# Attention and expert layer: the planner learns that engines share a PSUM bank one at a time

## The chip, the cores and the metric

The kernel runs on one core of a Trainium2 chip. The metric is the time of one execution on the device in microseconds (us). Three runs of the kernel before took 918.87, 920.80 and 922.08 us, a median of 920.8 us.

The names of the engines in profiles: PE is TensorE's matmul, PEld its weight load, DVE is VectorE, ACT is ScalarE, POOL is GpSimd and SP is SyncE, which here issues the DMAs.

## The reference

An attention over 8 batches, 8 heads, 576 positions and 64 channels is followed by a two-layer network on 4608 tokens of 512 channels (hidden width 2048). Half of the heads see the last 32 positions, the other half every 32nd.

```python
scores = scale * np.matmul(q, k.transpose(0, 1, 3, 2))
mask_local = (rel >= 0) & (rel < stride)
mask_strided = (rel >= 0) & (pos[None, :] % stride == pos[:, None] % stride)
scores = np.where(masks[None, :, :, :], scores, -1000000000.0)
attn = np.exp(scores - np.max(scores, axis=-1, keepdims=True))
attn = attn / (np.sum(attn, axis=-1, keepdims=True) + 1e-09)
x = np.matmul(attn, v)               # then (B * S, H * D)
h = x @ w_in
sp = np.maximum(h, 0.0) + np.log1p(np.exp(-np.abs(h)))
g = h * erf(sp)
return (g @ w_out).astype(np.float32)
```

## The kernel before

Every value of the network is split into a high part, which TensorE multiplies at full rate, and a low part for the rest; a product of two such values is three matmuls (high by high, high by low, low by high).

The work has four stretches. In the head (up to about 46 us) the attention of the first two batches is computed (`head`), while the weights arrive by DMA and are split. In the second stretch (to about 267 us) three chunks of 384 tokens go through the network tile by tile (`ftile`): mm1 fills a bank `h`, VectorE and ScalarE make the gate from it in some nine alternating steps (n1 to split_lo), and mm2 multiplies the result with `w_out`. Then come six phases of 512 tokens (`phase`), each of eight pair groups (`pair_group`), 48 in all, to about 834 us; the attention of the later batches runs between them (`quad`, `attend`, `products`). A last chunk of 384 tokens ends the kernel (`tail`).

A pair group computes two tiles of the hidden layer with seven products in place of eight, by a scheme of Strassen's kind. It uses two PSUM banks, g[0] and g[1], each with a left and a right half of 256 columns:

- mmA (TensorE) writes both halves of g[0], mmB both halves of g[1]; each is 12 matmuls of 256 columns.
- save1 (ScalarE) copies g[0] left into `tmp`. mix1 (VectorE) adds g[0] right and writes `tmp` (called `spare` in the profile).
- mix3 (VectorE) writes g[0] right from g[1] right. mix2 writes g[1] left, save2 (ScalarE) copies it, mix4 writes g[1] right.
- mmC (6 matmuls) adds to g[0] left; it needs save1 and mmB. mmD (6) adds to g[0] right; it needs mix3. mmE (6) adds to g[1] left; it needs save2 and mix4.

After that both banks are gated like the tiles of a chunk, with 512 columns, and mm2 takes the first 384 tokens of each (three blocks of three matmuls a tile), while the last 128 are put aside for mmL. In the profile mmA to mmE are L1229, mix1 to mix4 L1238, save1 and save2 L1244, mm2 is L1397 (in chunks L961), mmL L1272, mm1 L894; the gating steps on VectorE are L1347, L1358 and L1368 (in chunks L905, L929 and L935).

All operations are first recorded in a plan, with an engine, a duration that the author gave, the operations they come after and the buffers they use. Five PSUM banks are shared by all tiles of the tags in `SHARED` (`ps`, `s`, `t`, `h`, `g`, `d`). `ORDER`, a table of 4669 numbers, gives each engine a queue of its operations. `Plan.order` then lets the planned time run: at each step it asks `_ready` when the first operation of each queue could begin, starts the one that can begin earliest, and returns all operations by their planned start. In that order they are written into the program, with `keep_in_program_order`, and there the layer below puts in the semaphores: an instruction waits for those written before it with which it shares a buffer. While the planned TensorE has nothing to do before the first mm1, `order` fills in a warm matmul (L1525).

Of the kernel before, what the change touches and what calls it, by code (L numbers as in the profile page):

```python
# [65 lines left out]
class Buf:  # L66


    def __init__(self, tag, make):
        self.tag, self.make, self.users = tag, make, []  # L70
        self.tile = self.bank = None
# [29 lines left out]
SHARED, NBANK = {"ps", "s", "t", "h", "g", "d"}, 5  # L101


class Op:
    def __init__(self, eng, dur, emit, after, new, use, earliest):
        self.eng, self.dur, self.emit, self.earliest = eng, dur, emit, earliest
        self.after, self.new = list(after), list(new)
        self.start = self.end = None
        self.behind, self.slack = [], 0.0
        self.locks = eng == "pool" or eng == "dve" and emit.__name__ in TWO  # L110
        for b in self.new + list(use):
            b.users.append(self)

    def pools(self):
        return {p for b in self.new for p in ((b.tag, "bank") if b.tag in SHARED else (b.tag,))}


class Plan:

    ENGINES = ("pe", "act", "dve", "pool", "sp")
    SAME = {"pe": 0.0, "act": 0.14, "dve": 0.13, "pool": 0.1, "sp": 0.0}
    LATENCY = {"pe": 0.25, "act": 0.2, "dve": 0.15, "pool": 0.6, "sp": 0.1}
# [14 lines left out]
    def _ready(self, op, live, last):  # L140
        t = max([op.earliest, *(last[p] for p in op.pools())])
        if any(p.end is None for p in op.behind):
            return None
        for p in op.after:
            if p.end is None:
                return None
            t = max(t, p.end + (self.SAME if p.eng == op.eng else self.LATENCY)[op.eng])
        for i, b in enumerate(op.new):
            order = live.setdefault(b.tag, [])
            n = len(order) - self.bufs[b.tag] + sum(x.tag == b.tag for x in op.new[:i])  # L150
            if n >= 0:
                for u in order[n].users:
                    if u.end is None:
                        return None
                    t = max(t, u.end + (self.SAME if u.eng == op.eng else self.LATENCY)[op.eng])
        need = sum(b.tag in SHARED for b in op.new)
        if need:
            free = sorted(self._vacant(op.eng))
            if len(free) < need:
                return None  # L160
            t = max(t, free[need - 1][0])
        return t + op.slack
# [85 lines left out]
def attention_moe(  # L248
# [1286 lines left out]
    held, sync = None, mybir.DependencyInfo(mybir.DependencyClass.Sync, mybir.DependencyReason.DATA)  # L1535
    for op in plan.order(ORDER):
        for x in op.new:
# [142 lines left out]
```

## Time and profile before

| what | before |
|---|---|
| median of three runs | 920.8 us |
| profiled execution | 919.72 us |
| its span, from the first to the last instruction | 917.9 us |
| TensorE busy | 896.8 us, 98% |
| VectorE busy | 763.6 us, 83% |
| ScalarE busy | 637.5 us, 69% |
| granted TensorE clock, mean | 1.000 |
| chain that ended last | PE 72%, DVE 19%, ACT 6% |

The busy time of TensorE is a sum of pipelined matmuls with modelled ends; a matmul of 512 columns shows some 0.39 us, while the next one starts after 0.23 us. A stall therefore shows less in the busy share than in the distance between starts and in the idle time of the weight loads (PEld), which run ahead of the matmuls. A row such as `[0.27 <-DVE spare L1238]` says that the engine stood idle for 0.27 us before this instruction, and which instruction ended that.

### The profile page before, as it was taken

The numbers are of one execution on the slowest core, as the hardware profiler recorded it, in microseconds if no ns is written. First come the engines' busy times: TensorE is split into PE (matmuls) and PEld (weight loads), VectorE is DVE, ScalarE is ACT, GpSimd is POOL, SyncE is SP. The second block draws the span as 40 slices with busy tenths as digits, with TensorE's granted clock in tenths as the row PEclk, the third lists the DMA queues.
The fourth block names the chain that finished last, engine by engine and source line by source line (L and its number), as shares of the span: only waits on it lengthen the run. The fifth ranks groups of instructions, "written<-read, shape, count | busy, mean of one in ns | idle before, by whom it ended". The sixth has DMA issues, their size and how long they took to land.

```text
span 917.9 us, 20199 instructions
## 1 busy us (share of the span) xinstructions
PE 896.8 (98%) x7530; PEld 780.2 (85%) x7530; DVE 763.6 (83%) x1669; ACT 637.5 (69%) x1484; POOL 348.1 (38%) x208
## 2 busy tenths in 40 slices
PE   9999999999989999999999999999999999999998
PEld 7889999888878887888788888888888888888997
DVE  6899989998998888889988889888988986774453
ACT  4877777676766776686667776876677677775554
POOL 4631363156663435464354446524356131000000
PEclk9999999999999999999999999999999999999999
DMA  9987746536748654585646764856577646553531
GB/s 359 363 312 203 228 148 209 157 95 190 219 166 270 216 182 174 204 265 185 219 171 226 239 199 120 300 164 217 161 234 240 196 152 192 188 184 115 173 114 46
DMA packets 90721, 183.51 MB, mean 200 GB/s; under 512 B 8704, under 2 KB 37888, under 8 KB 90624
## 3 DMA queue, kind: packets, MB, share of 16 engines
q1 hardware_dynamic: 90480, 182.12, 61.0%
q8 instruction: 59, 0.97, 0.4%
q14 instruction: 38, 0.31, 0.1%
q10 hardware_dynamic: 144, 0.11, 0.0%
HBM read 151.53 MB, written 30.67 MB: 198 GB/s over the span
## 4 chain that ended last, share of the span: by engine, by line
PE 72%; DVE 19%; ACT 6%; issue 2%; DMA 1%; DVEq 0%; ACTq 0%
PE ps L1229 20%; PE eo L1397 14%; PE ps L894 12%; PE o L961 12%; PE ps L1272 5%; DVE ps L1238 2%; PE warm L1525 2%; DVE glo_t L1368 2%; ACT ga L1353 1%; DVE ps L774 1%; DVE ga L1347 1%; PE ps L618 1%; DVE ps L1358 1%; ACT spare L1353 1%; DVE spare L1347 1%
## 5 line engine op out<-in xcount | busy, mean ns | idle before, releaser
L1397 PE MATMUL eo<-pair,ghi_t 128*128 128x512 f32 x576 | 181.8, 397 | 0.0
L1229 PE MATMUL ps<-T,st 128*128 128x256 f32 x1152 | 160.4, 285 | 3.8 <-DVE ps L1238 3.2
L1229 PEld LDWEIGHTS ps<-T,st 128*128 128x128 f32 x1152 | 149.0, 191 | 12.6 <-DVE ps L1238 6.6
L1229 PE MATMUL ps<-B,st 128*128 128x256 f32 x864 | 130.3, 289 | 8.1 <-DVE ps L1238 2.5
L1229 PEld LDWEIGHTS ps<-B,st 128*128 128x128 f32 x864 | 115.0, 190 | 26.8 <-DVE ps L1238 9.6
L961 PE MATMUL o<-pair,ghi 128*128 128x512 f32 x384 | 121.0, 396 | 0.0
L659 POOL PARTITION_ALL_REDUCE su_True<-sm_True x36 | 90.4, 2533 | 64.0 <-ACT sm_True L653 20.1
L908 ACT ACTIVATE ga<-ga 128x384 f32<-128x384 f32 x192 | 98.4, 523 | 23.0 <-DVE ga L905 21.4
L1397 PE MATMUL eo<-pair,glo_t 128*128 128x512 f32 x288 | 112.3, 390 | 0.0
L1397 PEld LDWEIGHTS eo<-pair,ghi_t 128*128 128x128 f32 x576 | 99.3, 189 | 14.0
L1353 ACT ACTIVATE ga<-ga 128x512 f32<-128x512 f32 x144 | 91.1, 633 | 15.3 <-DVE ga L1347 13.2
L1353 ACT ACTIVATE spare<-spare 128x512 f32<-128x512 f32 x144 | 91.1, 633 | 9.9 <-DVE spare L1347 8.3
L659 POOL PARTITION_ALL_REDUCE su_False<-sm_False x36 | 90.5, 2560 | 19.2 <-ACT sm_False L653 7.9
L639 POOL PARTITION_ALL_REDUCE mx_False<-sm_False x36 | 51.2, 1452 | 117.4 <-DVE sm_False L633 108.2
L639 POOL PARTITION_ALL_REDUCE mx_True<-sm_True x36 | 51.5, 1443 | 111.0 <-DVE sm_True L633 47.2
L1238 DVE TENSOR_TENSOR ps<-ps,spare 128x256 f32<-128x256 f32 x144 | 61.6, 429 | 35.8 <-PE ps L1229 29.2
L905 DVE SCALAR_TENSOR_TENSOR ga<-ga,ps 128x384 f32<-128x384 f32 x128 | 69.4, 547 | 23.7 <-ACT ga L908 22.4
L961 PEld LDWEIGHTS o<-pair,ghi 128*128 128x128 f32 x384 | 70.1, 188 | 12.4 <-ACT ghi L932 0.5
L961 PE MATMUL o<-pair,glo 128*128 128x512 f32 x192 | 75.9, 395 | 1.1 <-DVE glo L935 1.1
L894 PE MATMUL ps<-xhi,pair 128*128 128x384 f32 x384 | 75.5, 338 | 1.2 <-DVE sm_False L633 1.1
L1347 DVE SCALAR_TENSOR_TENSOR ga<-ga,ps 128x512 f32<-128x512 f32 x96 | 65.1, 678 | 10.1 <-ACT ga L1353 9.9
L1244 ACT COPY spare<-ps 128x256 f32<-128x256 f32 x96 | 35.7, 372 | 54.3 <-DVE ps L1238 48.8
(128 smaller groups left out, 1751.4 us busy)
## 6 DMA issues: line engine op xcount, KB each, us to landing
st<-ws SPq DMA_DIRECT2D x152, 512.0 KB, 4.7
st<-ws SPq DMA_DIRECT2D x64, 256.0 KB, 4.2
words<-w_out SPq DMA_DIRECT2D x16, 512.0 KB, 6.8
words<-w_in SPq DMA_DIRECT2D x16, 512.0 KB, 7.1
ws<-pair SPq DMA_DIRECT2D x64, 128.0 KB, 3.7
qk_True<-qk_loc SPq DMA_DIRECT2D x18, 416.0 KB, 5.1
out<-eob SPq DMA_DIRECT2D x24, 256.0 KB, 4.1
qk_False<-qk_str SPq DMA_DIRECT2D x12, 472.0 KB, 5.5
```

Source lines behind the costliest of these rows:

```text
L639: yield nc.gpsimd.partition_all_reduce(mx[k][:, :cols], sm[k][:, :cols], P, ReduceOp.max)
L659: yield nc.gpsimd.partition_all_reduce(su[k][:, :cols], sm[k][:, :cols], P, ReduceOp.add)
L894: yield nc.tensor.matmul(ph[:, :CH], weights(s, cc, w, fs), x[cc // 2][:, cc % 2, :], start=(i == 0), stop=(i == len(terms) - 1))
L905: yield nc.vector.scalar_tensor_tensor(out=out, in0=in0, scalar=scalar, in1=in1, op0=op0, op1=op1)
L908: yield nc.scalar.activation(dst, src, func, bias=bias[i], scale=scale)
L961: yield nc.tensor.matmul(po[:, half], g[:, ts], wout[f][:, w, half], start=(f == fs0 and i == 0), stop=(f == fs1 and i == 2 and half.stop ...
L1229: yield nc.tensor.matmul(slot(m, i), st[q][:, b, k, w], blk[x][:, y, k], start=first and t == k == 0, stop=True, skip_group_check=True,)
L1238: yield nc.vector.tensor_tensor(out=out(), in0=slot(*psum), in1=tmp[:, part], op=op)
L1272: yield nc.tensor.matmul(dps[0][:, :], x, wout[f][:, w, :], start=f == 0 and i == 0, stop=f == NFC - 1 and i == 2,)
L1347: yield nc.vector.scalar_tensor_tensor(out=a.tile, in0=a.tile, scalar=scalar, in1=ph[:, :TT], op0=ALU.mult, op1=ALU.add)
L1353: yield nc.scalar.activation(a.tile, ph[:, :TT] if i == 0 else a.tile, AF.Tanh, bias=bias[i], scale=scale)
L1397: yield nc.tensor.matmul(po.tile, x[:, ts], wout[f][:, w], start=f == 0 and i == 0, stop=f == NFC - 1 and i == 2)
```

## The change

`_ready` gets a rule: an operation that uses a shared bank may not be planned to start before the operations of other engines that were already started on that tile have ended, whichever part of the bank they touch. Before, only the operations named in `after`, and the handing over of a bank to a new tile, were planned for. The program's semaphores keep such pairs apart in the order they are written, before as now. With the new rule another `ORDER` was sought, a permutation of the same 4669 numbers; 273 places hold the same number as before.

```diff
-ORDER = (5, 229, 4667, 4, 4668, 131, 249, 230, 9, 21, 250, 231,
...
+ORDER = (1, 5, 229, 4, 39, 4667, 230, 4668, 249, 131, 210, 6,
...
@@ -110,6 +110,7 @@
         self.locks = eng == "pool" or eng == "dve" and emit.__name__ in TWO
         for b in self.new + list(use):
             b.users.append(self)
+        self.banks = [b for b in use if b.tag in SHARED]
...
@@ -153,6 +154,10 @@
                     if u.end is None:
                         return None
                     t = max(t, u.end + (self.SAME if u.eng == op.eng else self.LATENCY)[op.eng])
+        for b in op.banks:
+            for u in b.users:
+                if u.end is not None and u.eng != op.eng:
+                    t = max(t, u.end + self.LATENCY[op.eng])
         need = sum(b.tag in SHARED for b in op.new)
         if need:
             free = sorted(self._vacant(op.eng))
```

All lines behind it have numbers that are 5 higher in the new kernel (L1229 is L1234, L1238 is L1243, L1397 is L1402).

The order of TensorE, in the last pair group of the first phase. `st0` to `st2` hold the group's weights: st0 is mmA (its second half is the first row here), st1 mmB, st2 with B21 mmC and with B22 mmD; the rows that write `eo` are mm2, three matmuls to a block. Before:

```order
L1229 MATMUL ps3_98<-T2_0_3532,st0_0_7_4442 128x256 x6
L1397 MATMUL eo0_0_3852<-pair26_1973,ghi_t0_10_4488 128x512 x2
L1397 MATMUL eo0_0_3852<-pair26_1973,glo_t0_10_4501 128x512
L1229 MATMUL ps0_95<-T3_0_3601,st1_0_7_4470 128x256 x6
L1229 MATMUL ps0_95<-T1_0_3434,st1_0_7_4470 128x256 x6
L1229 MATMUL ps3_98<-B21_0_3556,st2_0_7_4499 128x256 x6
L1229 MATMUL ps3_98<-B22_0_3647,st2_0_7_4499 128x256 x6
L1397 MATMUL eo2_0_3863<-pair26_1973,ghi_t0_10_4488 128x512 x2
L1397 MATMUL eo2_0_3863<-pair26_1973,glo_t0_10_4501 128x512
```

Now:

```order
L1234 MATMUL ps3_98<-T2_0_3543,st0_0_7_4448 128x256 x6
L1234 MATMUL ps2_97<-T3_0_3644,st1_0_7_4460 128x256 x6
L1234 MATMUL ps2_97<-T1_0_3471,st1_0_7_4460 128x256 x6
L1402 MATMUL eo1_0_3897<-pair26_1984,ghi_t0_10_4486 128x512 x2
L1402 MATMUL eo1_0_3897<-pair26_1984,glo_t0_10_4499 128x512
L1402 MATMUL eo0_0_3855<-pair26_1984,ghi_t0_10_4486 128x512 x2
L1402 MATMUL eo0_0_3855<-pair26_1984,glo_t0_10_4499 128x512
L1234 MATMUL ps3_98<-B21_0_3565,st2_0_7_4496 128x256 x6
L1234 MATMUL ps3_98<-B22_0_3557,st2_0_7_4496 128x256 x6
L1402 MATMUL eo2_0_3838<-pair26_1984,ghi_t0_10_4486 128x512 x2
L1402 MATMUL eo2_0_3838<-pair26_1984,glo_t0_10_4499 128x512
```

One block of mm2 stood between mmA and mmB and none between mmB and mmC; now none stands before mmB and two stand behind it. mmC and mmD follow each other as before, and behind them come mm2 and mmE.

The order of VectorE in the same group. The row that writes `spare` from `ps3` is mix1; those of the same line behind it are mix3, mix2 and mix4; L1347 and L1358 (now L1352 and L1363) are gating steps of other tiles. Before:

```order
L1358 TENSOR_TENSOR ps2_97<-ga_93,ps2_97 128x512
L1238 TENSOR_TENSOR spare_3651<-ps3_98,spare_3651 128x256
L1238 TENSOR_TENSOR ps3_98<-ps0_95,spare_3651 128x256
L1238 TENSOR_TENSOR ps0_95<-ps0_95,spare_3651 128x256
L1171 TENSOR_TENSOR B11_1_4567<-x01_3116,B11_1_4567 128x512
L1358 TENSOR_TENSOR ps1_96<-spare_3651,ps1_96 128x512
L1238 TENSOR_TENSOR ps0_95<-ps0_95,spare_3651 128x256
```

Now:

```order
L1243 TENSOR_TENSOR spare_3642<-ps3_98,spare_3642 128x256
L1352 SCALAR_TENSOR_TENSOR spare_3642<-spare_3642,ps4_99 128x512
L1243 TENSOR_TENSOR ps3_98<-ps2_97,spare_3642 128x256
L1243 TENSOR_TENSOR ps2_97<-ps2_97,spare_3642 128x256
L674 STREAM_TRANSPOSE tt_3_True_1_4567<-su0_3_True_1_4453 128x384
L1363 TENSOR_TENSOR ps1_96<-ga_93,ps1_96 128x512
L651 TENSOR_TENSOR sm0_3_True_2_4359<-sm0_3_True_2_4359,mx0_3_True_2_4517 128x384
L678 TENSOR_SCALAR r_3_True_1_4585<-tt_3_True_1_4567 128x12
L682 RECIPROCAL r_3_True_1_4585<-r_3_True_1_4585 128x12
L1243 TENSOR_TENSOR ps2_97<-ps2_97,spare_3642 128x256
```

mix1, mix3 and mix2 stand in the same sequence; a gating step now comes between mix1 and mix3, and four more rows between mix2 and mix4. What a row of one engine doesn't show is how it stands to the other engine's: in the program before, mix3 of this group is written behind mmC, now ahead of it. So it is in 35 of the 48 groups before and in 15 now; mmC follows directly on mmB in 30 groups before and in 13 now.

The number of warm matmuls before the first mm1 is 122 before and 115 now. No other instruction of TensorE, VectorE or ScalarE is added or taken away.

## Rows read from the trace of the kernel before

**Rows 1.** The page, part 1: engine, busy us (share of the span), instructions.
```profile
PE 896.8 (98%) x7530; PEld 780.2 (85%) x7530; DVE 763.6 (83%) x1669; ACT 637.5 (69%) x1484; POOL 348.1 (38%) x208
```

**Rows 2.** Waits of TensorE's weight loads, whole span: us in total, times, longest.
```profile
PEld ps L1229 <- DVE ps L1238: 16.2, 40, 1.5
...
PEld ps L1229 <- DVE spare L1238: 6.0, 14, 0.9
...
PEld ps L1229 <- issue: 3.0, 8, 0.9
```

**Rows 3.** Timeline, TensorE, one pair group: start, us, what [idle before <-releaser].
```profile
341.79 0.88 PE L1229 MATMUL ps<-B,st 128*128 128x256 f32 x6
342.50 0.88 PE L1229 MATMUL ps<-T,st 128*128 128x256 f32 x6
...
343.92 1.59 PE L1229 MATMUL ps<-T,st 128*128 128x256 f32 x12
345.77 0.97 PE L1229 MATMUL ps<-B,st 128*128 128x256 f32 x6 [0.27 <-DVE spare L1238]
347.27 0.98 PE L1229 MATMUL ps<-B,st 128*128 128x256 f32 x6 [0.53 <-DVE ps L1238]
```

**Rows 4.** Timeline, VectorE, the same stretch.
```profile
345.30 0.42 DVE L1238 TENSOR_TENSOR spare<-ps,spare 128x256 f32<-128x256 f32 x1
346.79 0.90 DVE L1238 TENSOR_TENSOR ps<-ps,spare 128x256 f32<-128x256 f32 x2 [1.07 <-PE ps L1229]
```

**Rows 5.** Timeline, weight loads, the same stretch.
```profile
345.77 0.77 PEld L1229 LDWEIGHTS ps<-B,st 128*128 128x128 f32 x6 [0.47 <-DVE spare L1238]
347.27 0.78 PEld L1229 LDWEIGHTS ps<-B,st 128*128 128x128 f32 x6 [0.73 <-DVE ps L1238]
```

**Rows 6.** Timeline, TensorE, another pair group.
```profile
598.35 0.63 PE L1397 MATMUL eo<-pair,ghi_t 128*128 128x512 f32 x2
...
599.05 0.62 PE L1397 MATMUL eo<-pair,ghi_t 128*128 128x512 f32 x2
...
599.74 1.59 PE L1229 MATMUL ps<-B,st 128*128 128x256 f32 x12
```

**Rows 7.** Timeline, VectorE, the same stretch.
```profile
598.15 0.39 DVE L1238 TENSOR_TENSOR spare<-ps,spare 128x256 f32<-128x256 f32 x1
598.64 0.90 DVE L1238 TENSOR_TENSOR ps<-ps,spare 128x256 f32<-128x256 f32 x2
```

**Rows 8.** Line L1238 by itself: count, ns min/median/max, first and last start.
```profile
L1238 DVE TENSOR_TENSOR ps<-ps,spare x144: 401/432/433, 278.2 to 834.3; 128x256 f32<-128x256 f32 x144
```

**Rows 9.** Timeline, ScalarE, the stretch of rows 3.
```profile
347.72 0.37 ACT L1244 COPY spare<-ps 128x256 f32<-128x256 f32 x1 [0.56 <-DVE ps L1238]
```

**Rows 10.** Timeline, all engines, 436 to 439 us.
```profile
436.24 2.78 POOL L659 PARTITION_ALL_REDUCE su_False<-sm_False  x1 [0.16 <-DVE tt_False L669]
...
436.57 1.58 DVE L673 TENSOR_SCALAR r_False<-tt_False 128x9 f32<-128x9 f32 x1
...
438.78 0.38 PE L1229 MATMUL ps<-T,st 128*128 128x256 f32 x1 [1.31 <-DVE ps L1238]
```

**Rows 11.** Timeline, TensorE, where the pair groups begin.
```profile
273.99 0.68 PE L618 MATMUL ps<-qk_False 64*64 64x54 f32 x30 [2.33 <-DVE glo L935]
...
275.90 1.70 PE L1229 MATMUL ps<-T,st 128*128 128x256 f32 x12 [0.34 <-DVE sm_False L633]
```

**Rows 12.** Chain that ended last, up to 47 us: shares, then start, us, what.
```profile
by line: PE warm L1525 34.7%; PE ps L488 17.0%; PE av L500 16.7%; PE ps L391 9.5%; PE ps L471 7.3%; PE ps L535 4.6%; PE ps L500 2.9%; DVE sm L415 2.5%; PE ps L376 1.0%; DVE xn L526 0.7%; issue 0.4%; DVE cap L1528 0.4%; DVE r L515 0.4%; DVE 
...
41.24 2.29 PE warm L1525 x21
```

**Rows 13.** Stretches: us, busy (x) of each engine, clock, DMA share, GB/s.
```profile
0.00:46.00 46.00, 44.94 (x519) 35.55 (x520) 35.18 (x86) 30.89 (x92) 24.00 (x19) 1.00 0.96 360
...
267.00:834.00 567.00, 552.72 (x4982) 478.66 (x4982) 482.18 (x1062) 398.88 (x923) 225.94 (x115) 1.00 0.63 203
```

**Rows 14.** Waits of VectorE, whole span: us in total, times, longest.
```profile
DVE ps L1238 <- PE ps L1229: 29.2, 36, 5.4
```

2 lines of the change are left out of this document (1 added, 1 removed).

## The prediction

> **What bounds the kernel now.** I read the page's busy times first, then who the matmul engine waits for, then two stretches of the timeline, and last the order of the instructions. TensorE is busy for 98% of the span, every other engine for less [rows 1], so time can be won only where TensorE does not start its next matmul in time. Its matmuls are pipelined and their ends are modelled, so I take the idle time of the weight loads: a load that has to wait delays its matmul by nearly as much. The summary of these waits names one line above all: the matmuls of L1229 (the pair groups, mmA to mmE) wait 16.2 us in 40 places for a VectorE step of L1238 that writes `ps` (mix2 to mix4) and 6.0 us in 14 places for the one that writes `spare` (mix1); 3.0 us in 8 places end by nothing that the profile names [rows 2]. These 25 us are the stock from which this change can draw.
>
> The group at 341.8 us shows what the waits are [rows 3, 4]. mmB starts at 343.92 with 12 matmuls; at the 0.72 us for six that the rows of mmA show (341.79 to 342.50), mmC could start at 345.35. It starts at 345.77: mix1 ends at 345.72 (345.30 + 0.42). mmC reads and writes only the left half of bank g[0], and mix1 reads its right half; the two share nothing but the bank, and still the matmul is held until the VectorE step is over. Then mix3 (first of the two at 346.79) begins only when mmC's last matmul has ended (345.77 + 0.97 = 346.74); again they share only the bank. mmD truly needs mix3 and starts at 347.27, 0.78 us after mmC could have let it in. So 1.2 us are lost, and the two loads show idle times of 0.47 and 0.73 us [rows 5], the same sum. The holds are in the program, in the order in which it was written out; the planner of before did not know them.
>
> The group at 594.1 us shows the other way [rows 6, 7]: after mmB two blocks of mm2 follow (598.35 and 599.05, 0.69 us each), mix1 and then mix3 (in the pair at 598.64, over at 599.54) run beside them, and mmC and mmD follow at 599.74 as one row of 12 matmuls without a gap.
>
> **The change part by part.** No instruction of the real work is added or removed; the rule gives the planner the holds that the chip already carries out, and the numbers of ORDER give another order. So the sum is made from the places that moved.
>
> 1. *mix3 ahead of mmC.* Matching the rows of the order with the trace, before has mix3 behind mmC in 35 of the 48 groups and before it in 13; the change has it behind in 15 and before it in 33. Directly after mmB, with no other block, mmC stands in 30 groups before and in 13 now. The pieces of the order in the section on the change show it: two blocks of mm2 went from both sides of the group to between mmB and mmC. Of the load waits, the 35 groups carry the 14 for mix1 (6.0 us), 26 of the 40 for `ps` (9.6 us, all before mmD; the second of rows 5 is one) and 1.4 us of smaller ones: 17.0 us, 0.49 us a group. The 13 groups carry 3.5 us, 2.2 of it among the 8 without a name: 0.27 us a group. Twenty groups change sides: 20 x 0.22 = 4.3 us less. Bounds: nothing, if the wait only moves on to mmE; 17 us, if all 33 groups are as smooth as the one at 594.1 and the other 15 get rid of half.
>
> 2. *mmE.* The other 14 of the 40 waits, 6.6 us, stand before mmE, which needs mix4. After mmB, the steps mix3, mix2, save2 and mix4 must run one after the other: three times 0.43 us on VectorE [rows 8] and 0.37 us for the copy on ScalarE [rows 9], about 1.8 us with hand-overs of 0.05 us as between mix1 and mmC. Beside them TensorE has mmC, mmD and what the order puts between: in 9 groups of before just one block (2.1 us in all), now in 1; over all groups 3.8 us before and 4.2 now. I take 2 us of the 6.6. Bounds: 3 us worse (these waits grow by half, as mmC comes later) and 5 us better; the longest single one, 1.31 us at 438.78, will not show a pattern [rows 10].
>
> 3. *The start of the pair groups.* At 273.99 the scores wait 2.33 us for a bank that a split_lo of L935 still holds, and mmB waits 0.34 us for a mask [rows 11]. In the new order the scores stand one block of mm2 (0.69 us) later behind the last mm1, and two blocks stand between them and mmB. I take 1.3 us; bounds 0 and 2.7.
>
> 4. *The head.* Up to the first mm1 at 45 us TensorE is never idle, because the planner fills its gaps with warm matmuls: they make 34.7% of the chain up to 47 us, and 21 of them take 2.29 us, 0.109 us each [rows 12]. There are 122 before and 115 now, with the same real work: 7 x 0.109 = 0.8 us less, if the data are there. The loads of the head stand in another order on SP's queue, whose transfers fill the DMA to 96% up to 46 us [rows 13]; 1 us worse to 1 us better.
>
> The tail is the same but for one block of mm2 moved by one mmL: nothing. The bursts of scores and products (45 and 42 blocks) are as many as before. Where mm2 blocks were taken from between mmC and mmD (0.60 us a group on average before, none now) mmD follows mmC at once, and what covers it is that mix3 is already done.
>
> One thing about VectorE speaks against step 1. In the window of the pair groups it is busy for 482 of 567 us [rows 13], and its waits for L1229 matmuls are 29.2 us in 36 places [rows 14]: at 346.79 everything behind mix3 stands still with it, the gating steps too [rows 4]. The Trainium skill, "PSUM — Partial Sum Buffer", section "Engine vs sequencer instructions", says that the queues of ScalarE, VectorE and GpSimd are strictly first in, first out; the trace agrees, with 1.07 us idle before that row. By that rule an earlier mix3 can hold up the gating of other tiles, which is the third rival below; by the row, mix3 waited for mmC as well as for mmB, and in the new order for mmB alone.
>
> Sum: 4.3 + 2 + 1.3 + 0.8 = 8.4 us. The profiled execution took 919.7 us (span 917.9 and 1.8 around it), so 911.3; it lies 1.1 us under the median of the runs, 920.8, which would make 912.4. I say 912.
>
> **The rivals.**
> *The waits are nearly all gone (903).* If a planner that knows the holds gets rid of them wherever another block is at hand, 15 groups keep 0.49 us and 33 keep none: 7.3 of 20.5 us, 13 less. With 3 of mmE and 2 of steps 3 and 4 it is 18 us. For it speaks the group at 594.1; against it that in before even the 13 groups with mix3 in front kept 0.27 us each.
> *The wait moves (920).* The blocks of mm2 that now stand behind mmB are no longer before mmA or mmE of the next group, and what mmC and mmD gain comes back before mmE, whose chain of 1.8 us starts at mmB's end in either order; or the holds were worth little since the search had covered them by chance. Then only step 4 is left, 0 to 2 us. For it: TensorE's work is the same and it is 98% busy; against it: the distance from mmB to mmE grew.
> *VectorE is held up (928).* mix3, written before mmC in 20 more groups, waits in VectorE's queue for mmB. At 0.81 us a wait (29.2 / 36) that is 16 us more of idle time on an engine with 85 us to spare in that window; if it falls on the gating chains just then needed, glo comes late and mm2 with it: 16 us lost for 8 won, 8 slower. It decides from where the idle time before L1238 passes about 40 us. Against it: in before the same queue stood still for mmB and mmC together.
>
> **How the numbers follow.** The forecast (906 to 917.5 by itself) gets 0.52, the first rival 0.14, the second 0.20, the third 0.14. A measurement of this kernel can tell about 0.3%, 2.8 us, from no change (the three runs lie from 918.9 to 922.1), so faster means under 918.0 and slower over 923.6. Faster: 0.52 and 0.14, less a little of the forecast's edge, 0.65; same 0.20; slower 0.15. The range from 902 to 923 leaves out some 0.06 below and 0.14 above.
>
> **What would show it.** Step 1: the waits of the weight loads of this line for the mix of `spare` fall from 6.0 to under 3 us, and those for `ps` from 16.2 to about 9. Step 2: what remains of these stands before mmE. Step 3: no wait over 2 us before scores around 270 us. Step 4: the first mm1 by 44.5 us. The forecast is wrong if the load waits of this line stay over 20 us, if the idle time before L1238 on VectorE passes 40 us, or if mm2 in the pair groups comes to wait several us for glo. VectorE's steps that are stretched beside GpSimd (the 1.58 us of L673 at 436.57, otherwise 0.17 us [rows 10]) can fall on other places by chance and are worth a us or two either way.

## The result and the profile after

The changed kernel takes 898.66 us, the median of 4 runs (898.15 to 899.59); the kernel before took 920.73 us on the same chips (4 runs). The ratio is 0.9763 with a 95% interval of 0.9744 to 0.9782: 22 us less. The forecast was 912 with a range from 902 to 923; the time lies below it. The profiled execution took 898.15 us, with a span of 896.3 (before 917.9).

The first part of the page of the kernel after, with engine, busy us (share of the span) and instructions, answers to [rows 1]:

```profile
PE 885.9 (99%) x7523; PEld 781.2 (87%) x7523; DVE 762.7 (85%) x1669; ACT 637.7 (71%) x1484; POOL 348.0 (39%) x208
```

The work is the same on every engine; there are seven warm matmuls fewer. The chain that ended last says where the time went:

```profile
PE 89%; DVE 7%; ACT 1%; POOL 1%; issue 1%; DMA 1%; DVEq 0%; POOLq 0%; ACTq 0%
```

Before it was PE 72%, DVE 19%, ACT 6%. The end is now set by TensorE's own work nearly all the way. The waits of its weight loads over the whole span (us in total, times, longest) answer to [rows 2]:

```profile
PEld ps L623 <- issue: 5.3, 15, 0.4
PEld ps L748 <- issue: 4.6, 13, 0.4
PEld o L966 <- DVE glo L940: 2.9, 4, 1.5
PEld ps L1234 <- DVE sm_False L638: 2.2, 2, 2.0
PEld L1530 <- DVE cap L1533: 2.2, 1, 2.2
...
PEld ps L1234 <- issue: 1.1, 3, 0.5
PEld ps L1234 <- DVE ps L1243: 1.0, 3, 0.5
...
PEld ps L1234 <- DVE spare L1243: 0.4, 1, 0.4
```

What is left at the top stands before scores (L623) and products (L748), 0.4 us at most in one place. The waits for a mix, 16.2 and 6.0 us before, are 1.0 and 0.4 us: 20.8 us less, and the span is 21.6 us shorter. By stages, from the first instruction of each in the two traces: the first mm1 at 45.0 us in both; the first pair group at 267.5 before and 265.9 now; from there to the end of the last mmE 569.5 and 549.7 us; the tail 80.9 and 80.8. So 19.8 us came from the pair groups and 1.6 from the stretch ahead of them.

The group of [rows 3] stands at 336.67 us now. TensorE's rows in it (start, us, what):

```profile
336.67 0.88 PE L1234 MATMUL ps<-B,st 128*128 128x256 f32 x6
337.38 2.32 PE L1234 MATMUL ps<-T,st 128*128 128x256 f32 x18
339.54 0.63 PE L1402 MATMUL eo<-pair,ghi_t 128*128 128x512 f32 x2
...
340.24 0.62 PE L1402 MATMUL eo<-pair,ghi_t 128*128 128x512 f32 x2
...
340.93 1.59 PE L1234 MATMUL ps<-B,st 128*128 128x256 f32 x12
```

and VectorE's beside them, which answer to [rows 4]:

```profile
338.76 0.42 DVE L1243 TENSOR_TENSOR spare<-ps,spare 128x256 f32<-128x256 f32 x1 [0.41 <-ACT spare L1249]
339.10 0.68 DVE L1352 SCALAR_TENSOR_TENSOR spare<-spare,ps 128x512 f32<-128x512 f32 x1
339.74 0.90 DVE L1243 TENSOR_TENSOR ps<-ps,spare 128x256 f32<-128x256 f32 x2
```

mmB's last matmul begins by 339.54, mix3 and mix2 run under the two blocks of mm2 (339.74 to 340.64), and mmC and mmD go through as one row of 12 at 340.93. The 1.2 us lost here before are gone.

The sum of all waits of the weight loads is 55.9 us before and 32.6 now, and span less sum is 862.0 and 863.7: what the span lost is nearly all waits. That sum is the yardstick for the experiments below. Of the load waits of the pair groups the table gives two counts: those whose row names a mix, and all that stand before mmC, mmD and mmE, whatever the row names.

| profiled execution | span | load waits, all | naming a mix | before mmC, mmD, mmE | span less all |
|---|---|---|---|---|---|
| before | 917.9 | 55.9 | 22.3 | 27.2 | 862.0 |
| after | 896.3 | 32.6 | 1.4 | 3.6 | 863.7 |
| old table, rule added | 923.2 | 61.2 | 17.4 | 29.6 | 862.0 |
| new table, no rule | 898.4 | 34.8 | 2.2 | 5.4 | 863.6 |
| new table, mmC directly behind mmB | 924.3 | 59.1 | 10.0 | 27.9 | 865.2 |
| the same in the first 24 groups | 906.8 | 43.6 | 7.1 | 14.5 | 863.2 |
| new table, cover rotated by a group | 911.1 | 51.5 | 6.1 | 18.6 | 859.6 |
| old table, mmC ahead of mmD | 918.3 | 56.3 | 9.6 | 24.5 | 862.0 |
| that, fitted from its trace | 923.4 | 62.8 | 4.4 | 15.6 | 860.6 |
| old table, short mixes | 906.9 | 40.1 | 9.3 | 12.2 | 866.9 |
| new table, short mixes | 896.6 | 33.3 | 0.4 | 2.7 | 863.3 |

The last column hardly moves, by some 4 us either way. The count by names falls short wherever mmC stands behind mix3: a row names the step that ended last on the engines waited for, and that can be a step that mmC does not need. The fifth column goes with the time: 23.6 us of these waits went with the change, and the span is 21.6 us shorter. The fitted old table is the exception, second slowest with 15.6 us, because new waits stand elsewhere in it.

### The profile page after: what moved, and what is told of

It is laid out like the page before. It is cut to its first block, busy times and chain, and to the rows that moved or that the text cites. A ratio compares the mean times of both kernels' runs of the same rounds, so it can differ in the third digit from the quotient of the medians.

```text
span 896.3 us, 20189 instructions
## 1 busy us (share of the span) xinstructions
PE 885.9 (99%) x7523; PEld 781.2 (87%) x7523; DVE 762.7 (85%) x1669; ACT 637.7 (71%) x1484; POOL 348.0 (39%) x208
## 4 chain that ended last, share of the span: by engine, by line
PE 89%; DVE 7%; ACT 1%; POOL 1%; issue 1%; DMA 1%; DVEq 0%; POOLq 0%; ACTq 0%
PE ps L1234 26%; PE eo L1402 21%; PE ps L899 13%; PE o L966 13%; PE ps L1277 7%; PE ps L623 2%; PE ps L748 2%; PE warm L1530 1%; POOL su_False L664 1%; PE ps L493 1%; PE av L505 1%; DVE ga L910 1%; PE ps L396 1%; DMA st<-ws 1%; PE ps L505 1%
## 5 line engine op out<-in xcount | busy, mean ns | idle before, releaser
L1402 PE MATMUL eo<-pair,ghi_t 128*128 128x512 f32 x576 | 182.3, 398 | 0.0
L1234 PE MATMUL ps<-T,st 128*128 128x256 f32 x1152 | 158.4, 284 | 2.3 <-DVE sm_False L638 1.9
L1234 PEld LDWEIGHTS ps<-T,st 128*128 128x128 f32 x1152 | 148.7, 191 | 7.6 <-DVE sm_False L638 2.2
L1234 PEld LDWEIGHTS ps<-B,st 128*128 128x128 f32 x864 | 116.7, 191 | 10.2 <-ACT spare L1358 1.5
L1234 PE MATMUL ps<-B,st 128*128 128x256 f32 x864 | 124.6, 285 | 0.6 <-ACT spare L1358 0.2
L1402 PEld LDWEIGHTS eo<-pair,ghi_t 128*128 128x128 f32 x576 | 100.1, 190 | 14.8
L1402 PE MATMUL eo<-pair,glo_t 128*128 128x512 f32 x288 | 112.5, 391 | 0.0
L1358 ACT ACTIVATE ga<-ga 128x512 f32<-128x512 f32 x144 | 90.8, 631 | 13.1 <-DVE ga L1352 11.1
L1358 ACT ACTIVATE spare<-spare 128x512 f32<-128x512 f32 x144 | 91.1, 633 | 12.2 <-DVE spare L1352 10.4
L644 POOL PARTITION_ALL_REDUCE mx_False<-sm_False x36 | 51.5, 1461 | 94.3 <-DVE sm_False L638 86.9
L1243 DVE TENSOR_TENSOR ps<-ps,spare 128x256 f32<-128x256 f32 x144 | 61.3, 427 | 21.4 <-PE ps L1234 15.7
L1352 DVE SCALAR_TENSOR_TENSOR ga<-ga,ps 128x512 f32<-128x512 f32 x96 | 65.3, 680 | 12.5 <-ACT ga L1358 11.9
L1277 PE MATMUL ps<-pair,keep 128*128 128x512 f32 x288 | 71.4, 392 | 0.0
```

Source lines behind the costliest of these rows:

```text
L644: yield nc.gpsimd.partition_all_reduce(mx[k][:, :cols], sm[k][:, :cols], P, ReduceOp.max)
L1234: yield nc.tensor.matmul(slot(m, i), st[q][:, b, k, w], blk[x][:, y, k], start=first and t == k == 0, stop=True, skip_group_check=True,)
L1243: yield nc.vector.tensor_tensor(out=out(), in0=slot(*psum), in1=tmp[:, part], op=op)
L1277: yield nc.tensor.matmul(dps[0][:, :], x, wout[f][:, w, :], start=f == 0 and i == 0, stop=f == NFC - 1 and i == 2,)
L1352: yield nc.vector.scalar_tensor_tensor(out=a.tile, in0=a.tile, scalar=scalar, in1=ph[:, :TT], op0=ALU.mult, op1=ALU.add)
L1358: yield nc.scalar.activation(a.tile, ph[:, :TT] if i == 0 else a.tile, AF.Tanh, bias=bias[i], scale=scale)
```

## The experiments

The theories. One: the new table gives each pair group its cover, that is, work of TensorE behind mmB in just the time that the mixes need, and by that takes the waits away. Two: the rule itself in `_ready` does it. Three: the gain lies elsewhere (head, start of the groups). Four, formed later: the old table's VectorE sequence brings the mixes late, so a better place for mmC only moves the wait.

**The rule without the table, and the table without the rule.** Each half of the change alone: in the first the kernel after has the numbers of before, in the second the kernel before has the numbers of after.

```diff
-ORDER = (1, 5, 229, 4, 39, 4667, 230, 4668, 249, 131, 210, 6,
+ORDER = (5, 229, 4667, 4, 4668, 131, 249, 230, 9, 21, 250, 231,
```

> The new rule with the old table of numbers: each engine keeps its old sequence, and in 27 of 325 bank tiles engines now follow each other in another sequence (mix3 written ahead of mmC in 18 groups, 13 before). Theory one (cover: what counts is how much TensorE work stands ahead of mmC, mmD and mmE while the VectorE steps they wait for run): that cover is as before, so 914 to 921 us and over 18 us of load waits of the pair-group matmuls for the mix steps. Theory two (the rule itself: who goes first on a bank is what makes the gain): under 905 us. Theory three (the new order is better in many other places, the banks are incidental): as before, 919 to 922.

> The new table of numbers without the rule: 323 of 325 bank tiles have the sequence of the changed kernel. Theories one and three: 898 to 900 us, as the changed kernel. Theory two: over 910 us.

The rule on the old table: 925.14 us, ratio 1.0047 (1.0035 to 1.0059), 4.7 us slower and above what any theory had expected. The table without the rule: 899.35, ratio 0.9762 (0.9737 to 0.9786), the whole gain. Theory two falls: beside the new table the rule does nothing for the time, and beside the old one it costs. Whatever it is worth, it was worth in the search for the table; whether a search without it would have found as good a table was not tried, since the search is no part of the kernel.

**mmC moved, in the new table and in the old.** In the new table mmC goes directly behind mmB in the 35 groups where it stood later; in the old table (with the rule) it goes from behind mmB to directly ahead of mmD in 33 groups. For a group of the new table, in TensorE's queue (in the old table the move goes the other way):

```diff
 mmB
+mmC
 mm2
 mm2
-mmC
 mmD
```

> The changed kernel with mmC put directly behind mmB on TensorE in the 35 groups where other blocks stood between; nothing else in the table changes. mmC then is written ahead of mix3 in 37 groups, as in the kernel before (35). Theory one: mmC, mmD and mmE wait again, load waits for the mix steps over 12 us in place of 1.4, and 908 to 918 us. Theory three: 898 to 902 us, load waits of a few us.

> The old table with the new rule, and mmC put directly ahead of mmD on TensorE in the 33 groups where other blocks stood between the two, so that these now stand between mmB and mmC; nothing else changes. Theory one: half of the gain or more, 904 to 914 us, load waits for the mix steps falling from 22 to under 12 us. Theory three: 917 to 922 us.

The new table without its cover: 925.79 us, ratio 1.0053 (1.0037 to 1.0069), 27 us lost by moving one step, more than the 9 to 19 that theory one expected; 27.9 us of waits stand before mmC, mmD and mmE again. Theory three asked for 898 to 902 here and falls; so it does by the stages above, 19.8 us in the pair groups.

The old table with the cover: 920.37, ratio 0.9996 (0.9983 to 1.0008). That is 4.8 us less than the old table with the rule alone, its nearest neighbour, but nothing won over the kernel before. Theory one had expected 904 to 914; it lies in the 917 to 922 of theory three, which the other run rules out. Yet on average mmC begins 1.41 us after mmB's end (1.47 in the kernel after, 0.64 before). Its load waits show why:

```profile
PEld ps L1234 <- DVE ps L1243: 9.6, 14, 1.4
PEld ps L1234 <- issue: 7.3, 15, 0.9
...
PEld ps L1234 <- ACT spare L1358: 5.5, 7, 1.3
```

By the move mmC is written behind mix3 in 40 groups, in place of 18 with the rule alone, and so it has to wait for mix3 where mix3 is late. In 24 groups mmC's load begins within 0.25 us of the end of its mix3, after 14.3 us of waits in all; the rows name `issue` for 13 of these and another tile's step of ScalarE for most of the rest. The wait moved from mmD to mmC.

So in the new table the cover is needed, and in the old one a cover of the same average is not enough. The group at 571.05 us of the kernel after and the same group at 583.35 with mmC directly behind mmB show the first. After, three blocks of mm2 from 574.61 stand behind mmB, and mmD and mmC follow as one row:

```profile
573.18 1.59 PE L1234 MATMUL ps<-T,st 128*128 128x256 f32 x12
574.61 0.63 PE L1402 MATMUL eo<-pair,ghi_t 128*128 128x512 f32 x2
...
576.67 1.60 PE L1234 MATMUL ps<-B,st 128*128 128x256 f32 x12
```

With mmC directly behind mmB:

```profile
585.59 1.59 PE L1234 MATMUL ps<-T,st 128*128 128x256 f32 x12
...
587.43 0.42 DVE L1243 TENSOR_TENSOR spare<-ps,spare 128x256 f32<-128x256 f32 x1
587.95 0.90 DVE L1243 TENSOR_TENSOR ps<-ps,spare 128x256 f32<-128x256 f32 x2
...
588.92 0.77 PEld L1234 LDWEIGHTS ps<-B,st 128*128 128x128 f32 x6 [1.95 <-ACT keep L1367]
588.95 0.95 PE L1234 MATMUL ps<-B,st 128*128 128x256 f32 x6 [1.78 <-DVE ps L1243]
...
592.00 1.05 PE L1402 MATMUL eo<-pair,ghi_t 128*128 128x512 f32 x2
```

mmC stands still for 1.78 us until the mixes are over at 588.85 (its load's row names ScalarE's `keep`, another tile's step), and the blocks that were its cover come behind it and cover nothing. The 1.05 us of the last row, 0.63 elsewhere, belong to the section on the hardware.

**The same move in the first half of the groups.** mmC directly behind mmB in the first 24 groups alone (16 move).

> The changed kernel with mmC moved directly behind mmB in the first 24 of the 48 groups alone (16 groups move; all 35 cost 27 us). In the run with all of them these three phases took 2.2, 2.2 and 4.2 us longer, the last three 9.9, 4.6 and 4.5. If what a group loses is lost there and neither won back nor carried on: 907 us (905 to 909). If later groups win it back because the other engines have run ahead: 899 to 902. If a disturbed group throws the ones behind it off the table's fit as well: over 912.

908.76 us, ratio 0.9875 (0.9858 to 0.9892). The first three phases take 4.0, 2.5 and 4.2 us longer than after, the other three 0.3, 0.0 and -0.6. What the moved groups lose is lost there; nothing is won back or carried on.

**Is it the average cover, or the cover of each group?** The new table, with the number of blocks between mmB and mmC taken from the next group (35 groups change; 77 blocks stand there in place of 88, and mix3 is written ahead of mmC in 33 groups as in the kernel after). A group with two blocks whose neighbour has none:

```diff
 mmB
+mmC
 mm2
 mm2
-mmC
```

> The changed kernel with the number of blocks between mmB and mmC of each group replaced by that of the next group, as far as a group has so many: 35 groups change, the counts stay the same in sum but for 11 blocks (77 for 88), and mix3 is written ahead of mmC in 33 groups as in the changed kernel. Averages as in the changed kernel, fit per group gone. Theory of averages (my step 1: the share of groups with mix3 in front and the mean cover decide): 898 to 903 us. Theory of fit: late steps of 8 us and more, 907 to 920 us.

913.88 us, ratio 0.9928 (0.9905 to 0.9951). With the same count of groups on either side of the forecast's step 1, and 11 blocks fewer between mmB and mmC, 15 of the 22 us are lost, and 15 us of waits before mmC, mmD and mmE are back (18.6 for 3.6). The place of mmC has to fit its own group.

**The old table fitted by its trace.** In the old table with mmC ahead of mmD, mmC, mmD and mmE go one to three blocks later in the 23 places where that trace shows them waiting for a mix.

```diff
 mmB
-mmC
 mm2
+mmC
 mmD
```

> The kernel of the last run (old table, mmC ahead of mmD), with mmC, mmD or mmE put one to three blocks later on TensorE only in those groups where the trace of that run shows that TensorE waited for the step's mix; 23 places. Theory one in its stricter form (fit: each matmul step must stand behind its mix in its own group, averages do not help): half of its 17 us of late steps go, 909 to 915 us. Theory four (the old sequence of VectorE is what makes the mixes late, so the waits only move on): 918 to 922 us.

925.45 us, ratio 1.0053 (1.0033 to 1.0073), slower than either theory expected. Its load waits:

```profile
PEld ps L1234 <- issue: 6.7, 12, 0.9
...
PEld eo L1402 <- DVE glo_t L1373: 4.6, 8, 1.5
PEld ps L1234 <- DVE ps L1243: 4.4, 9, 0.8
...
PEld ps L1234 <- DVE keep L1373: 2.8, 5, 1.1
```

The waits before mmC, mmD and mmE fell by 9.0 us (24.5 to 15.6). Those before mm2 rose from nothing to 8.0, those before mmA and mmB from 4.5 to 9.9, and those before scores and products from 15.9 to 18.9: each block that was pulled into a group was missed elsewhere. In these two runs a new place in TensorE's sequence, with VectorE's sequence kept, did not mend the old table. That fits theory four; no run changed the old VectorE sequence alone, so for it this is the only evidence.

**mix1 off the bank.** In the kernel before, and later in the kernel after, mix1 adds the first half of its SBUF tile to itself; the addition of g[0] right is left out.

```diff
+        def mix1():
+            yield nc.vector.tensor_tensor(out=tmp[:, 1], in0=tmp[:, 0], in1=tmp[:, 0], op=ALU.add)
+
-        d1 = add("dve", td, stt("mix1", lambda: tmp[:, 1], (0, 1), 0), [c1], [], [g[0], tmp])
+        d1 = add("dve", td, mix1, [c1], [], [tmp])
```

> The kernel before, with mix1 reading its SBUF operand twice in place of the right half of bank g[0]: one addition is left out, so that mix1 and mmC no longer share a bank; order and all else as before. It measures one hold by itself. Theory one (the holds on the banks that the old plan did not know are what TensorE waits for): the 6.0 us of load waits before mmC that end with mix1 go, and since mix3 and mmD come earlier too, 911 to 916 us. Theory three (the gain is elsewhere): 919 to 922 us.

> The changed kernel with mix1 adding the first half of its SBUF tile to itself in place of the right half of the first bank (that addition is left out). It is the counterpart of the same edit on the kernel before, where it was worth nothing. Theory one (the table already covers mix1): 898 to 899.5 us, no change. If holds of mix1 on the bank still cost something on other engines: under 896.

The old table: 919.88 us, ratio 0.9992 (0.9982 to 1.0001), though its 6.0 us of waits for mix1 are gone. I read that first as a wait that moves on to mmD. The new table showed that the edit is not clean: 906.56 us, ratio 0.9844 (0.9816 to 0.9872), 8 us slower than without it, where no change was expected. In the old table the row of mix1 (count, ns min/median/max) is

```profile
L1257 DVE TENSOR_TENSOR spare<-spare x48: 360/420/1976, 277.3 to 827.0; 128x256 f32<-128x256 f32 x48
```

and in the new one, in the list of costly groups (busy us, mean ns)

```profile
L1262 DVE TENSOR_TENSOR spare<-spare 128x256 f32<-128x256 f32 x48 | 32.4, 676 | 5.9 <-ACT spare L1249 5.6
```

where mix1 with its bank takes 385 to 426 ns there. So the same edit without the sum, a constant written in its place:

```diff
-            yield nc.vector.tensor_tensor(out=tmp[:, 1], in0=tmp[:, 0], in1=tmp[:, 0], op=ALU.add)
+            yield nc.vector.memset(tmp[:, 1], 0.5)
```

> The kernel before with mix1 writing a constant into its SBUF tile in place of the sum (the sum is left out), so that it neither reads the bank nor, as the SBUF sum of the earlier run did, waits beside GpSimd (there 16 of 48 took 0.56 to 1.98 us in place of 0.42, 11 us of VectorE in all). If the hold of mix1 on the bank costs TensorE its 6.0 us of waits and the stretched sums hid the gain: 913 to 916 us. If the wait only moves on to mmD, which needs mix3, as that run showed: 918 to 921. If VectorE's shorter queue lets the other mixes come earlier as well: under 911.

> The changed kernel with the same edit. The SBUF sum made it 8 us slower (906.6), against nothing on the kernel before. If that came from the stretched sums (17 of 48, up to 1.85 us, 12 us more of VectorE): 896 to 899 us here. If it came from mix1 running at another time than the table was fitted to: over 902.

All 48 take 272 ns now. The old table: 915.56 us, ratio 0.9934 (0.9911 to 0.9958), 5.9 us faster than before, about the 6.0 us of waits of [rows 2], with an interval from 4 to 8. The new table: 898.92, ratio 0.9751 (0.9732 to 0.9770), no change. So the hold of mix1 on the shared bank did cost time of that order, the new table has it covered, and my first reading of the earlier run was wrong: there the waits of mmD for mix3 rose from 9.8 to 14.0 us, here they are 9.3. The profiled execution of the old table, at 917.41 us the slowest of its four, shows only 2.7 us of load waits less. What part of the gain is mix1's own length, 0.15 us shorter here and 7 us of VectorE in all, was not separated.

**Short mixes.** Each of the four mixes works on 64 of its 256 columns, in either kernel; the other sums are left out.

```diff
-            yield nc.vector.tensor_tensor(out=out(), in0=slot(*psum), in1=tmp[:, part], op=op)
+            yield nc.vector.tensor_tensor(out=out()[:, :64], in0=slot(*psum)[:, :64], in1=tmp[:, part, :64], op=op)
```

> The kernel before, with each of mix1 to mix4 working on 64 of its 256 columns (three quarters of the sums are left out), so that each takes some 0.2 us less and the chain mix3, mix2, save2, mix4 some 0.5 us less; the order of all instructions is that of before. Theory one (the kernels differ by what TensorE's loads wait for the mixes, and by nothing else): the 22 us of such waits fall to under 6, and the time comes to 901 to 907 us. Theory four (VectorE's whole sequence in the old table is late, the mixes only show it): the waits go to mm2 and to the next groups as in the fitted order, and the time stays over 912. Together with the same edit on the changed kernel it tells what is left between the two tables when the mixes cost little.

> The changed kernel with the same edit: each mix works on 64 of its 256 columns. Theory one: there are only 1.4 us of waits for the mixes left to win, so 896 to 899 us, and its distance to the kernel before with this edit shrinks from 22 us to under 10. Theory four: VectorE, which also has some 35 us less to do, lets TensorE's other waits shrink too: under 894, and the distance between the two tables stays over 15 us.

A mix takes 0.23 us in place of 0.43. The old table comes down to 908.60 us, ratio 0.9880 (0.9859 to 0.9902); the new one to 897.13, ratio 0.9751 (0.9733 to 0.9769). The distance between the tables halves, to 11.5 us (under 10 was expected), and 9.5 us of it are what the old table still waits before mmC, mmD and mmE (12.2 against 2.7). I had expected 901 to 907 for the old table: mixes of half the length still leave 12.2 of the 27.2 us of waits, so their length is not all of it; what holds the rest was not taken apart. The new table wins next to nothing from cheaper mixes, the old one 12.6 us.

**A step of VectorE moved in the new table.** At 282.57 us mmB waits 1.90 us for a mask that stands behind two gating steps.

```diff
+mask of the scores (L638, 128x288)
 L1352 ga
 L1352 spare
-mask of the scores (L638, 128x288)
 L985 ob
```

> The changed kernel with one VectorE step moved: the mask of the scores at 279.92 us, which lets go of the bank that mmB needs, goes ahead of two gating steps (each 0.60 us later by that, the mask 1.2 us earlier). mmB waits 1.90 us for it at 282.57 there, and behind that wait TensorE's granted clock stands at half for 3.4 us, some 1.7 us of work at 2.4 GHz. If the wait shrinks to 0.8 us and the clock then stays up: 1.1 + 1.7 = 2.8 us less, 895.9 us. If the clock falls all the same: 897.5. If the gating steps then come late for mm2: 898 to 900, no gain.

899.85 us, 5 runs from 898.16 to 901.54: nothing won over the kernel after. The rows are of the execution that took 901.54:

```profile
280.69 1.69 PE L1234 MATMUL ps<-T,st 128*128 128x256 f32 x12 [0.71 <-DVE sm_False L638]
283.72 0.95 PE L1234 MATMUL ps<-B,st 128*128 128x256 f32 x6 [1.33 <-DMA st<-ws]
...
286.08 0.80 PE L1402 MATMUL eo<-pair,glo_t 128*128 128x512 f32 x1 [0.95 <-DVE glo_t L1373]
```

mmB's wait shrank to 0.71 us; mmC then waited 1.33, and mm2 0.95 for glo. mmC's row names the weights' DMA, its load's row a gating step of ScalarE; by the trace save1, the step of ScalarE that mmC needs, was over at 282.82, while the weights landed at 283.58, just ahead of the load at 283.69. So it was the weights. In the kernel after they land at 284.17 and mmC begins at 284.44: there was little for an earlier mmB to win. VectorE's rows show where the wait for glo came from:

```profile
284.77 0.42 DVE L1243 TENSOR_TENSOR spare<-ps,spare 128x256 f32<-128x256 f32 x1 [1.49 <-PE ps L1234]
285.12 0.45 DVE L638 TENSOR_TENSOR sm_False<-ps,cap 128x288 f32<-128x288 f32 x1
285.48 0.55 DVE L1373 TENSOR_TENSOR glo_t<-ps,ghi_t 128x384 fp32r<-128x384 f32 x1
```

mix1 now stands behind mmC on the bank and is held for 1.49 us, and the step that writes glo stands behind mix1; in the kernel after, mix1 is over at 284.05, before mmC begins at 284.44. The half clock that stands behind these waits lasted 6.8 us here and 3.4 in the kernel after (last section). No version with all the sums that is faster than the kernel after was found.

## Why the forecast was wrong

The direction was right, and so was the stock: the load waits in the pair groups are what was won, 23.6 of the 27.2 us before mmC, mmD and mmE. The size was not.

**Step 1 is the step that failed.** It valued a group by a class, mix3 ahead of mmC (0.27 us of waits) or behind (0.49), and let 20 groups change class: 4.3 us. The waits before mmC and mmD fell from 20.5 us to 3.1, 17.4 less, a little over the upper bound that I had given the step and four times its value. The 0.27 us themselves were a matter of cover: of the 3.5 us in these 13 groups, 3.3 are mmC waiting for the mix3 written ahead of it, in 7 places. In the kernel after a group waits 0.07 us in the first class (2.4 us in 33 groups) and 0.04 in the second (0.65 in 15). The class did not carry the price; the fit of the cover to its own group did, as the rotated cover shows: the same classes cost 0.31 and 0.35 us a group there (10.4 us in 33 groups, 5.3 in 15). An average over the groups of a table that had not been planned for these holds did not carry over to one that had.

**Step 2** took 2 us of the 6.6 before mmE; 6.1 went (0.52 us remain, in one wait), above its bound of 5. mmE begins as late behind mmB's end as before (4.19 us on average, before 4.09), but mix4 is over earlier: 3.09 us after mmB's end, before 3.46. mix3 is over earlier by as much, 1.15 us after mmB's end, before 1.57.

**Step 3** came to nothing in its own place. From the first mmA to the mmA of the third group it is 23.33 us before and 23.31 now, with one block of mm2 fewer in it. The wait of 2.33 us before the scores [rows 11] is gone, as its sign said, but mm2 waits 1.07 us for glo before 270.97 and mmB 1.90 us for a mask before 282.57, with the half clock behind it. The 1.6 us won ahead of the first pair group look like the step's 1.3, but that is luck: no term of the sum stood there.

**Step 4** gave nothing for 0.8: the first mm1 begins at 45.0 us as before. There are seven warm matmuls fewer, but the first one starts 1.1 us later, since it waits 2.19 us for `cap` (1.06 before), which is more than the 0.8 us that seven of them take.

**The rivals.** The first, that the waits are nearly all gone, was the right mechanism, and even it left 7.3 us in 15 groups where 0.65 remained. Against it I had held the 0.27 us of the 13 groups of before, the number that step 1 rests on. The second, the wait that moves, is false for the kernel after and true for the attempts to better one engine's sequence by hand: mmC moved in the old table, the fitted old table and the moved mask. The third fell: VectorE's idle time for those matmuls went down and not up, and the price that I took for a wait, the mean of [rows 14], did not come:

```profile
DVE ps L1243 <- PE ps L1234: 15.7, 17, 6.0
```

It was 29.2 us in 36 places. The strict queues that the Trainium skill tells of ("PSUM — Partial Sum Buffer", section "Engine vs sequencer instructions") are real, as the held mix1 of the last experiment shows, with glo behind it and mm2 0.95 us late; but in the kernel after such waits of VectorE became fewer, not more.

## What to carry to other kernels

When a plan learns of a hold that the program's semaphores already carry out, price the whole stock of waits that it causes as a serious outcome, and not only the difference between positions that the old plan happened to have. Span less the sum of TensorE's load waits stayed put over the kernels here (860 to 867 us), so the question for a forecast is which waits go. Count them by the place where they stand: the name in a row is the step that ended last, and in the old table with mmC moved it missed more than half of the waits before mmC, mmD and mmE. And do not expect to carry a good order over piece by piece: one step moved in the fitted table cost more than the whole gain (mmC) or won nothing (the mask).

## What the runs showed of the hardware

**A stretched sum of two SBUF operands.** mix1 from PSUM and SBUF takes 385 to 426 ns in the kernel after in all 48 places. With both operands in SBUF 16 of 48 took 557 to 1976 ns in the old table and 17 of 48 590 to 1851 in the new, some 12 us of VectorE in either. All 33 of them ran beside a PARTITION_ALL_REDUCE of GpSimd (another 16 touched one and were not stretched). The form with PSUM ran beside one in 27 of its 48 places in the kernel after and was never stretched, and a constant written to the same place always took 272, beside one or not. The Trainium skill, "GPSIMD Engine Reference", section "1. Specifications", names contention between GpSimd and VectorE instructions with two SBUF inputs; the rows agree with it. The 1.58 us of [rows 10] stood beside the same step of GpSimd, but that instruction has one SBUF tensor input, and the case of two does not cover it. An edit that takes an operand out of PSUM is therefore no neutral experiment.

**The clock after a wait.** In the kernel after TensorE stands still for 1.90 us until 282.57, and the granted clock (the column before the DMA share) falls to half, 1.2 GHz, soon after it has begun again:

```profile
281.00:282.50 1.50, 0.00 (x0) 0.00 (x0) 1.50 (x4) 1.01 (x3) 0.00 (x0) 1.00 0.99 336
282.50:284.00 1.50, 1.43 (x10) 1.43 (x11) 1.50 (x5) 1.42 (x4) 1.31 (x2) 0.89 0.99 387
284.00:285.50 1.50, 1.50 (x8) 1.50 (x8) 1.22 (x4) 1.03 (x3) 1.38 (x1) 0.50 0.36 141
285.50:287.50 2.00, 2.00 (x10) 1.71 (x9) 1.54 (x5) 0.37 (x1) 0.00 (x0) 0.60 0.75 198
287.50:289.00 1.50, 1.50 (x12) 1.37 (x11) 1.02 (x3) 1.03 (x3) 0.00 (x0) 1.00 1.03 388
```

That is 0.33 + 1.5 + 1.6 = 3.4 us at half speed, 1.7 us of work lost. Behind the 1.78 us of the moved mmC it was the same:

```profile
584.00:588.90 4.90, 3.17 (x24) 2.84 (x23) 4.76 (x11) 4.35 (x10) 2.48 (x2) 1.00 0.92 273
...
590.30:593.20 2.90, 2.90 (x8) 2.30 (x7) 0.61 (x2) 0.11 (x1) 0.00 (x0) 0.50 0.14 54
```

Not every such wait does it: the 2.33 us before 273.99 in the kernel before [rows 11] left the clock at full.

```profile
271.50:274.00 2.50, 0.17 (x9) 0.04 (x3) 2.43 (x5) 1.62 (x6) 1.99 (x1) 1.00 0.69 272
274.00:276.00 2.00, 1.66 (x34) 1.13 (x34) 2.00 (x5) 0.00 (x0) 0.70 (x1) 1.00 0.05 10
```

Nor did the wait of 1.90 us before mmB at 283.63 in the run with mmC directly behind mmB, the same wait as that of the kernel after: its clock stayed at full. And with the mask moved, three shorter waits (0.71, 1.33 and 0.95 us) were followed by half a clock all the same, for longer:

```profile
285.50:287.50 2.00, 1.41 (x4) 0.90 (x5) 1.97 (x6) 0.37 (x1) 0.00 (x0) 0.52 0.93 366
287.50:289.00 1.50, 1.50 (x7) 1.40 (x7) 1.05 (x3) 0.42 (x1) 0.00 (x0) 0.50 0.19 69
```

The clock rises again at 292.39 us there, so it stood at half for 6.8 us. A wait of TensorE can cost its own length and 1.7 us more, here once 3.4, and no row here tells beforehand which one will.
